# Collecting the outputs of a decode block in one PSUM bank, with one copy, a four-row store and a VectorE transpose for the second layer norm

## The chip, the cores and the metric

The kernel runs on one core of one Trainium2 chip. The metric is the device time of an execution in microseconds (us), and the median over several executions is quoted. "Span" is the time from the first to the last recorded event of the core in the trace. It is about 1.8 us less than the device time. The effects in this study are about 1 us in 410, so every ratio below is between executions on the same chip in the same session; the profiles, and a few times that are said to be of another session, come from several chips.

In the profile PE is TensorE, the matrix unit, and PEld its loads of the stationary operand; DVE is VectorE, ACT ScalarE, POOL GpSimd, and SP issues the transfers (DMA), which 16 DMA engines carry out. PSUM is the memory, of 128 partitions in banks, into which PE adds up its products. The "granted clock" is the share of its full clock that PE was given. LN2 is the second layer norm. A transfer has "landed" when the last of its completion signals is recorded in the trace.

## The reference

It is one decode step (one token) of a transformer block: a layer norm, attention over a cache of 65,536 positions, the residual, a second layer norm, and a gated feed-forward network. All inputs are bf16.

```python
B, Sq, D = 1, 1, 1024
Hq, Hkv, Sk, Dh = 32, 4, 65536, 128        # attention
F = 3584                                   # feed-forward
x = A_x
h  = x + attention(layernorm(x), k_cache, v_cache, wq, wo)      # o @ wo
hn = layernorm(h)
h2 = h + (gelu(hn @ w_gate) * (hn @ w_up)) @ w_down
return h2                                  # (1, 1, 1024) bf16
```

## The kernel before

Keys, values and weights are streamed through a ring of large buffers by one DMA queue, in a fixed order. `w_down` comes last, in five pieces of 14, 7, 4, 2 and 1 "chunks". A chunk is 128 rows of `w_down`, 256 KB. The change touches what happens after the attention projection, and the end.

A product with `w_down` can be laid out in two ways. As a *wide row*, the activation vector is the stationary operand and the weights move through PE, so the 1024 outputs lie along the free dimension of a few partitions. As *columns*, each 128x128 block of weights is loaded as the stationary operand and one column comes out, so the outputs lie across 128 partitions. The kernel used wide rows for the first 21 chunks, spread over four column groups of 32 so that four chunks add up side by side, and columns for the last seven. It joined the two by summing over partitions with one-column matmuls against a vector of ones, which also turns a row into columns.

```python
def row_mm(banks, stat, w2, c, first, last):          # wide row: chunk c in column group c % 4
    g = c % 4
    for s in range(DS):                               # DS = 2 halves of 512 columns
        mm(banks[s][32 * g:32 * g + 32, :], stat, w2[:, s * 512:(s + 1) * 512], first, last,
           loaded=(s > 0), tile_position=(0, 32 * g)) # the second half reuses the loaded weights
# ... attention output rows -> at_ps, copied to at_r [128, 2, 512] f32 ...
hc_ps = ps_t.tile([P, DC], F32, name="hc_ps", tag="T")
for s in range(DS):
    for c in range(DC):                               # 16 column sums: LN2's layout (p c)
        mm(hc_ps[64 * s:64 * s + 64, c:c + 1], at_r[:, s, c::DC], ones_f[:, 0:1], True, True,
           tile_position=(0, 64 * s))
h_pc = const.tile([P, DC], F32, name="h_pc")
nc.vector.tensor_tensor(out=h_pc[:], in0=hc_ps[:], in1=x_pc[:], op=ALU.add)
hn_bf = const.tile([P, DC], BF16, name="hn_bf")
layernorm_cols(h_pc[:], hn_bf[:], "ln2")
hnz = padded(rows, hn_bf[:], DC, "hnz")

def cp_sum(row, add, name):                           # 16 column sums: the output's layout (c p)
    ps = ps_t.tile([P, 4, DS], F32, name=name + "_ps", tag="T")
    for b in range(4):
        for s in range(DS):
            mm(ps[:, b, s:s + 1], row[:, s, b * P:(b + 1) * P], ones_f[:, 0:1], True, True)
    # ... the sums plus `add`, as t [128, 8] ...
h_cp = cp_sum(at_r, x_cp, "h_cp")
# ... gate and up products (they need hnz), GELU -> act_bf [128, 28] ...
sizes = [14, 7, 4, 2, 1]
NW = 21
for sz in sizes:
    wv = load(wd_v[:, c0:c0 + sz, :], "wd_sb")
    for cc in range(sz):
        c = c0 + cc
        if c < NW:
            row_mm(d_ps, actz[:, c, :], wv[:, cc, :], c, c < 4, c + 4 >= NW)
            continue
        for j in range(DC):                           # the last 7 chunks as columns
            mm(dl_ps[:, j:j + 1], wv[:, cc, j * P:(j + 1) * P], act_bf[:, c:c + 1], False, False,
               skip_group_check=True)
    c0 += sz
    if c0 == NW:                                      # rows of 21 chunks -> columns
        d_r = rows.tile([P, DS, 512], F32, name="d_r")
        for s in range(DS):
            evac(d_r[:, s, :], d_ps[s][:], s)
        hd_cp = cp_sum(d_r, h_cp, "hd_cp")
nc.vector.tensor_tensor(out=o_col[:], in0=dl_ps[:], in1=hd_cp[:], op=ALU.add)
oT_ps = ps_t.tile([DC, P], BF16, name="oT_ps", tag="T")
tr(oT_ps[:], o_col[:], ident_bf[:])                   # transpose on PE: [128, 8] -> [8, 128]
o_row = rows.tile([DC, P], BF16, name="o_row")
nc.vector.tensor_copy(out=o_row[:], in_=oT_ps[:])
nc.sync.dma_start(out=out[0, 0].rearrange("(c p) -> c p", p=P), in_=o_row[:])
```

Of the kernel before, what the change touches and what calls it, by code (L numbers as in the profile page):

```python
# [9 lines left out]
ALU = mybir.AluOpType  # L10
AX = mybir.AxisListType
BF16 = mybir.dt.bfloat16
F32 = mybir.dt.float32
PSUM = bass.MemoryType.PSUM
# [3 lines left out]
def kernel(  # L18
# [13 lines left out]
    nc = tc.nc  # L32
    P = 128
    D = A_x.shape[-1]
# [3 lines left out]
    rep = Hq // Hkv  # L38
    F = B_w_gate.shape[1]
    DC = D // P  # L40
    FC = F // P
# [13 lines left out]
    NS = Hkv * 4  # L55
    W0 = 32
# [3 lines left out]
    lead = ctx.enter_context(tc.tile_pool(name="lead", bufs=1))  # L60
    ones_f = lead.tile([P, P], F32, name="ones_f")
# [2 lines left out]
    sel = lead.tile([P, 32], F32, name="sel")  # L64
    hmask = lead.tile([P, rep], F32, name="hmask")
    x_pc = lead.tile([P, DC], F32, name="x_pc")
    x_cp = lead.tile([P, DC], F32, name="x_cp")
    x_row = lead.tile([DC, P], BF16, name="x_row")
    ident_bf = lead.tile([P, P], BF16, name="ident_bf")
    x_pc_bf = lead.tile([P, DC], BF16, name="x_pc_bf")  # L70
    xn_bf = lead.tile([P, DC], BF16, name="xn_bf")
    neg_half = lead.tile([P, 1], F32, name="neg_half")
    oT_all = lead.tile([P, Hq], BF16, name="oT_all")
    used = sum(-(-b // 32) * 32 for b in (4 * P, 4 * P, 2 * (W0 + NS * P), 128, 4 * rep, 4 * DC, 4 * DC, 2 * P, 2 * P,
                                          2 * DC, 2 * DC, 4, 2 * Hq))
    lead.tile([P, (-(used + 128)) % 4096], mybir.dt.uint8, name="lead_pad")
    chpool = ctx.enter_context(tc.tile_pool(name="chpool", bufs=NBUF))
# [46 lines left out]
    def mm(out, lhsT, rhs, start, stop, loaded=False, tile_position=None, skip_group_check=False):  # L124
        t = nc.tensor
        if not loaded:
            return pe(t.matmul(out, lhsT=lhsT, rhs=rhs, start=start, stop=stop, tile_position=tile_position,  # L127
                               skip_group_check=skip_group_check))
        op = t.add_instruction(mybir.InstMatmult(  # L129
            name=nc.get_next_instruction_name(), engine=t.engine, start_tensor_calc=start, stop_tensor_calc=stop,  # L130
            tile_size=(lhsT.shape[0], lhsT.shape[1]), tile_position=tile_position or (0, 0), ldweights=False,
            bass_skip_group_check=skip_group_check,
            ins=[t.lower_ap(rhs), t.lower_ap(lhsT, for_matmul_weights=True)], outs=[t.lower_ap(out, opt=True)]))
        reuses.add(op.ins.name)
        return pe(op)

    def tr(out, in_, identity):
        pe(nc.tensor.transpose(out=out, in_=in_, identity=identity))  # L138
# [9 lines left out]
    WB = max(1, CW // HD)  # L148
    assert HD <= CW and DC % WB == 0
    nc.scalar.dma_start(out=x_pc_bf[:], in_=A_x[0, 0].rearrange("(p c) -> p c", c=DC))  # L150
    nc.scalar.dma_start(out=x_row[:], in_=A_x[0, 0].rearrange("(c p) -> c p", p=P))
    wq_tiles = []
    for c0 in range(0, DC, WB):
        wv = load(wq_v[:, c0:c0 + WB, :], "wq_sb")
# [40 lines left out]

    nc.vector.tensor_copy(out=x_pc[:], in_=x_pc_bf[:])
    layernorm_cols(x_pc[:], xn_bf[:], "ln1")
    xT_ps = ps_m.tile([P, DC], BF16, name="xT_ps", tag="misc")
    tr(xT_ps[:], x_row[:], ident_bf[0:DC, 0:DC])
    nc.vector.tensor_copy(out=x_cp[:], in_=xT_ps[:])  # L200

    def padded(pool, vec, ncols, name, tag=None):
        t = pool.tile([P, ncols, 32], BF16, name=name, tag=tag or name)
        nc.gpsimd.memset(t[:], 0.0)
        nc.vector.tensor_copy(out=t[:, :, 0], in_=vec)
        return t
# [7 lines left out]
    def evac(dst, src, k):  # L214
        if k % 2 == 0:
            nc.vector.tensor_copy(out=dst, in_=src)  # L216
        else:
            nc.scalar.copy(out=dst, in_=src)
# [175 lines left out]
    actx.close()  # L394
    rows = ctx.enter_context(tc.tile_pool(name="rows", bufs=1))
    ps_w = ctx.enter_context(tc.tile_pool(name="ps_w", bufs=4, space=PSUM))
    ps_t = ctx.enter_context(tc.tile_pool(name="ps_t", bufs=3, space=PSUM))
    DS = D // 512

    def row_bank(name):  # L400
        return ps_w.tile([P, 512], F32, name=name, tag="w")

    def row_mm(banks, stat, w2, c, first, last):
# [3 lines that stand above are left out]
               loaded=(s > 0), tile_position=(0, 32 * g))  # L407
# [6 lines left out]
    for wc in range(Hq // WN):  # L414
        wv = load(wo_v[:, wc * WN:(wc + 1) * WN, :], "wo_sb")
        for cc in range(WN):
            c = wc * WN + cc
            row_mm(at_ps, o2z[:, c, :], wv[:, cc, :], c, c < 4, c + 4 >= Hq)
    at_r = rows.tile([P, DS, 512], F32, name="at_r")
    for s in range(DS):  # L420
        evac(at_r[:, s, :], at_ps[s][:], s)
    hc_ps = ps_t.tile([P, DC], F32, name="hc_ps", tag="T")
    for s in range(DS):
        for c in range(DC):
            mm(hc_ps[64 * s:64 * s + 64, c:c + 1], at_r[:, s, c::DC], ones_f[:, 0:1], True, True,
               tile_position=(0, 64 * s))
    h_pc = const.tile([P, DC], F32, name="h_pc")
    nc.vector.tensor_tensor(out=h_pc[:], in0=hc_ps[:], in1=x_pc[:], op=ALU.add)
    hn_bf = const.tile([P, DC], BF16, name="hn_bf")
    layernorm_cols(h_pc[:], hn_bf[:], "ln2")  # L430
    hnz = padded(rows, hn_bf[:], DC, "hnz")

    def cp_sum(row, add, name):
        ps = ps_t.tile([P, 4, DS], F32, name=name + "_ps", tag="T")
        for b in range(4):
            for s in range(DS):
                mm(ps[:, b, s:s + 1], row[:, s, b * P:(b + 1) * P], ones_f[:, 0:1], True, True)
        t = rows.tile([P, DC], F32, name=name)
        nc.vector.tensor_tensor(out=t[:].rearrange("p (s b) -> p b s", b=4), in0=ps[:],
                                in1=add[:].rearrange("p (s b) -> p b s", b=4), op=ALU.add)  # L440
        return t

    h_cp = cp_sum(at_r, x_cp, "h_cp")

    assert F <= CW and FC == 28
    GB = CW // F
# [55 lines left out]

    wd_v = B_w_down.rearrange("(p c) n -> p c n", p=P)
    sizes = [14, 7, 4, 2, 1]
    NW = 21
    assert sum(sizes) == FC
    actz = padded(rows, act_bf[:, 0:NW], NW, "actz")
    d_ps = [row_bank("d_ps") for _ in range(DS)]
    dl_ps = ps_m.tile([P, DC], F32, name="dl_ps", tag="misc")
    nc.vector.memset(dl_ps[:], 0.0)  # L510
    o_col = rows.tile([P, DC], BF16, name="o_col")
    c0 = 0
    for sz in sizes:
        wv = load(wd_v[:, c0:c0 + sz, :], "wd_sb")
        for cc in range(sz):
            c = c0 + cc
            if c < NW:
                row_mm(d_ps, actz[:, c, :], wv[:, cc, :], c, c < 4, c + 4 >= NW)
                continue
            for j in range(DC):  # L520
                mm(dl_ps[:, j:j + 1], wv[:, cc, j * P:(j + 1) * P], act_bf[:, c:c + 1], False, False,
                   skip_group_check=True)
        c0 += sz
        if c0 == NW:
            d_r = rows.tile([P, DS, 512], F32, name="d_r")
            for s in range(DS):
                evac(d_r[:, s, :], d_ps[s][:], s)
            hd_cp = cp_sum(d_r, h_cp, "hd_cp")
    nc.vector.tensor_tensor(out=o_col[:], in0=dl_ps[:], in1=hd_cp[:], op=ALU.add)
    oT_ps = ps_t.tile([DC, P], BF16, name="oT_ps", tag="T")  # L530
    tr(oT_ps[:], o_col[:], ident_bf[:])
    o_row = rows.tile([DC, P], BF16, name="o_row")
    nc.vector.tensor_copy(out=o_row[:], in_=oT_ps[:])
    nc.sync.dma_start(out=out[0, 0].rearrange("(c p) -> c p", p=P), in_=o_row[:])


# [28 lines left out]
```

## Time and profile before

| what | value |
|---|---|
| time, first three executions | 410.66 us (410.0 to 410.76) |
| time of the profiled execution | 411.24 us |
| span of the profiled execution | 409.5 us |
| data read | 173.02 MB |
| last weights landed (estimate below) | about 404.1 us |
| last weights landed to end of span | 5.3 us |

The load queue q1 is busy for 98.1% of the span, so the kernel is bound by data, except at its end.

The transfers view of the kernel before has one line for each kind of transfer, with its size and its time from issue to landing.

```profile
wd_sb<-in_B_w_down_dram SPq DMA_DIRECT2D x1, 256.0 KB, 13.3
```

This is the last piece of `w_down`. It was issued at 390.83 us, so it landed at about 404.1. The windows view of the kernel before agrees. Its columns are: the window and its length; busy time of PE, PEld, DVE, ACT and POOL with counts of instructions; the granted PE clock; the DMA share; and GB/s.

```profile
403.00:404.00 1.00, 1.00 (x6) 1.00 (x6) 0.00 (x0) 0.00 (x0) 0.00 (x0) 0.50 0.34 131
404.00:405.00 1.00, 1.00 (x8) 1.00 (x8) 0.00 (x0) 0.00 (x0) 0.00 (x0) 0.50 0.00 0
```

No data moves after 404, but PE is fully busy. The timeline of the kernel before shows with what. Each line has the start, the duration, the engine, source line and operation, output and input, count, and, in brackets, the idle time before it and what ended that.

```profile
366.72 0.18 DVE L205 COPY hnz<-hn_bf 128x8 bf16<-128x8 bf16 x1
...
370.35 1.04 PE L129 MATMUL wu_ps<-wu_sb,hnz 128*32 128x512 bf16 x7 [2.25 <-DMA wu_sb<-in_B_w_up_dram]
...
400.98 0.69 DVE L216 COPY d_r<-d_ps 128x512 f32<-128x512 f32 x1 [7.95 <-PE d_ps L129]
...
401.72 3.36 PE L127 MATMUL hd_cp_ps<-ones_f,d_r 128*128 128x1 f32 x16 [0.79 <-DVE d_r L216]
...
404.95 1.63 PE L127 MATMUL dl_ps<-act_bf,wd_sb 128*128 128x1 bf16 x56
...
406.62 0.17 DVE L529 TENSOR_TENSOR o_col<-dl_ps,hd_cp 128x8 bf16<-128x8 f32 x1 [1.32 <-PE dl_ps L127]
...
406.84 0.27 PE L138 MATMUL oT_ps<-ident_bf,o_col 128*8 128x128 bf16 x1 [0.26 <-DVE o_col L529]
407.14 0.21 DVE L533 COPY o_row<-oT_ps 8x128 bf16<-8x128 bf16 x1 [0.36 <-PE oT_ps L138]
407.44 0.37 SPq L534 DMA_DIRECT2D out_dram<-o_row  x1
```

The 16 column sums hold PE for 3.36 us and the 56 last matmuls queue behind them. PE is therefore late for the last weights, and the store is issued 3.3 us after they landed.

### The profile page before, as it was taken

How to read it: one execution, taken by the hardware profiler on the slowest of the kernel's cores; microseconds unless marked ns; L12 is line 12 of the kernel's file. 1: busy time of each engine (PE TensorE's matmuls, PEld its weight loads, DVE VectorE, ACT ScalarE, POOL GpSimd, SP SyncE). 2: the span in 40 equal slices, each digit the busy share in tenths (PEclk: the TensorE clock that was granted, in tenths of full speed). 3: DMA queues.
4: the chain of work that ended last, by engine and by line, in shares of the span. 5: the costliest groups of instructions: out<-in, count | busy, mean ns of one | idle time of the engine just before them, and what ended most of it. 6: DMA issues, size and time to landing. Idle time of an engine off the chain costs nothing.

```text
span 409.5 us, 2725 instructions
## 1 busy us (share of the span) xinstructions
PE 307.7 (75%) x1521; PEld 70.6 (17%) x732; DVE 202.6 (49%) x189; ACT 45.5 (11%) x68; POOL 7.2 (2%) x17
## 2 busy tenths in 40 slices
PE   0356397769997788898966869977867997875666
PEld 0111011111110111111111121110112111360224
DVE  1118989876683678646464958182753001110111
ACT  1010000050000041000002220000051000000000
POOL 2000000000000000000000000000010000100000
PEclk9965778969999989899989998999768899866666
DMA  8999999999999999999999999999999999999993
GB/s 359 410 461 410 453 416 442 427 439 432 415 451 416 455 411 451 419 448 423 439 431 426 445 414 450 419 445 423 448 423 434 435 426 445 419 432 429 439 413 151
DMA packets 6669, 173.20 MB, mean 423 GB/s; under 512 B 896, under 2 KB 896, under 8 KB 1152
## 3 DMA queue, kind: packets, MB, share of 16 engines
q1 hardware_dynamic: 6496, 173.02, 98.1%
q8 instruction: 9, 0.15, 0.1%
q10 hardware_dynamic: 160, 0.00, 0.0%
q14 instruction: 4, 0.03, 0.0%
HBM read 173.02 MB, written 0.00 MB: 423 GB/s over the span
## 4 chain that ended last, share of the span: by engine, by line
DMA 46%; PE 30%; DVE 18%; ACT 4%; issue 2%; SPq 0%; ACTq 0%; DVEq 0%
DMA k_sb<-in_A_k_cache_dram 32%; DVE k_sb L259 12%; PE acc_ps L129 10%; DMA wu_sb<-in_B_w_up_dram 8%; DMA wd_sb<-in_B_w_down_dram 6%; PE qk_ps L127 6%; PE qk_ps L129 6%; PE acc_ps L127 4%; DVE mx L280 2%; ACT sc L279 2%; DVE pT L304 1%; ACT pe_r L301 1%; PE o_ps L127 1%; DVE acc_sb L330 1%; ACT acc_sb L332 1%
## 5 line engine op out<-in xcount | busy, mean ns | idle before, releaser
L259 DVE STREAM_TRANSPOSE k_sb<-k_sb 128x2048 uint32<-128x2048 uint32 x64 | 142.1, 2278 | 33.8 <-DMA k_sb<-in_A_k_cache_dram 33.8
L127 PE MATMUL qk_ps<-k_sb,wsel 128*128 128x512 bf16 x256 | 104.7, 409 | 37.5 <-DVE k_sb L259 25.2
L129 PE MATMUL acc_ps<-v_sb,pT 128*128 128x512 bf16 x384 | 111.3, 401 | 0.0
L129 PE MATMUL qk_ps<-k_sb,wsel 128*128 128x512 bf16 x256 | 104.2, 407 | 0.0
L127 PE MATMUL acc_ps<-v_sb,pT 128*128 128x512 bf16 x128 | 51.4, 402 | 0.0
L127 PEld LDWEIGHTS <-wsel 128*128 128x128 bf16 x256 | 26.1, 102 | 143.4 <-issue 123.7
L280 DVE TENSOR_REDUCE mx<-qk_ps 128x1 f32<-128x1024 f32 x16 | 19.5, 1220 | 44.9 <-ACT sc L279 44.9
L279 ACT COPY sc<-qk_ps 128x1024 f32<-128x1024 f32 x16 | 16.2, 1012 | 201.9 <-PE qk_ps L129 201.9
L127 PEld LDWEIGHTS <-pT 128*128 128x128 bf16 x128 | 13.6, 106 | 98.3 <-issue 98.2
L304 DVE STREAM_TRANSPOSE pT<-pe_r 128x1024 bf16<-128x1024 bf16 x16 | 19.0, 1227 | 6.2 <-ACT pe_r L301 6.2
L330 DVE COPY acc_sb<-acc_ps 32x512 f32<-32x512 f32 x8 | 5.4, 672 | 32.8 <-PE acc_ps L129 32.7
L301 ACT ACTIVATE pe_r<-sc,nbias 128x1024 bf16<-128x1024 f32 x16 | 18.2, 1140 | 14.3 <-DVE nbias L296 13.5
L332 ACT COPY acc_sb<-acc_ps 32x512 f32<-32x512 f32 x8 | 4.6, 578 | 62.0 <-DVE acc_sb L330 61.9
L127 PE MATMUL q_ps<-wq_sb,xnz 128*32 128x512 bf16 x32 | 5.2, 625 | 7.9 <-DMA wq_sb<-in_A_wq_dram 7.9
L127 PE MATMUL ln_tot<-ln_s,ones_f 128*128 128x1 f32 x8 | 2.3, 352 | 10.8 <-DVE ln_s L177 8.9
L127 PE MATMUL o_ps<-sel,acc_sb 128*128 128x8 f32 x32 | 5.1, 288 | 6.7 <-DVE rl L344 5.9
L138 PE MATMUL mxT_ps<-ident_f,mx 128*1 128x128 f32 x4 | 1.3, 321 | 10.8 <-DVE mx L285 10.8
L127 PE MATMUL wg_ps<-wg_sb,hnz 128*32 128x512 bf16 x32 | 6.4, 591 | 3.8 <-DMA wg_sb<-in_B_w_gate_dram 3.1
L129 PE MATMUL wu_ps<-wu_sb,hnz 128*32 128x512 bf16 x40 | 7.3, 586 | 2.3 <-DMA wu_sb<-in_B_w_up_dram 2.3
L216 DVE COPY wg_ev<-wg_ps 128x512 f32<-128x512 f32 x1 | 0.7, 692 | 14.9 <-PE wg_ps L127 14.9
L216 DVE COPY q_ev<-q_ps 128x512 f32<-128x512 f32 x1 | 0.7, 692 | 14.0 <-PE q_ps L129 14.0
L127 PE MATMUL d_ps<-wd_sb,actz 128*32 128x512 bf16 x21 | 3.4, 538 | 4.0 <-DMA wd_sb<-in_B_w_down_dram 4.0
(116 smaller groups left out, 110.6 us busy)
## 6 DMA issues: line engine op xcount, KB each, us to landing
k_sb<-in_A_k_cache_dram SPq DMA_DIRECT2D x16, 4096.0 KB, 33.7
v_sb<-in_A_v_cache_dram SPq DMA_DIRECT2D x16, 4096.0 KB, 36.8
wq_sb<-in_A_wq_dram SPq DMA_DIRECT2D x2, 4096.0 KB, 16.7
wo_sb<-in_A_wo_dram SPq DMA_DIRECT2D x2, 4096.0 KB, 30.3
wg_sb<-in_B_w_gate_dram SPq DMA_DIRECT2D x2, 3584.0 KB, 31.6
wu_sb<-in_B_w_up_dram SPq DMA_DIRECT2D x2, 3584.0 KB, 32.7
wd_sb<-in_B_w_down_dram SPq DMA_DIRECT2D x1, 3584.0 KB
wd_sb<-in_B_w_down_dram SPq DMA_DIRECT2D x1, 1792.0 KB, 24.6
```

Source lines behind the costliest of these rows:

```text
L127: return pe(t.matmul(out, lhsT=lhsT, rhs=rhs, start=start, stop=stop, tile_position=tile_position, skip_group_check=skip_group_check))
L129: op = t.add_instruction(mybir.InstMatmult(name=nc.get_next_instruction_name(), engine=t.engine, start_tensor_calc=start, stop_tensor_calc ...
L138: pe(nc.tensor.transpose(out=out, in_=in_, identity=identity))
L216: nc.vector.tensor_copy(out=dst, in_=src)
L259: dv(nc.vector.transpose(out=kt[:, c * w:(c + 1) * w], in_=kt[:, c * w:(c + 1) * w]))
L279: ac(nc.scalar.copy(out=sc[:], in_=flat))
L280: dv(nc.vector.tensor_reduce(out=state[("mx", g)][:, li:li + 1], in_=flat, axis=AX.X, op=ALU.max))
L301: ac(nc.scalar.activation(out=pe_r[:], in_=state.pop(("sc", g, li))[:], func=ACT.Exp, bias=nbias[:, 0:1], scale=scale, accum_out=lpart[:, ...
L304: dv(nc.vector.transpose(out=pT[:].rearrange("p m c -> p (m c)"), in_=pe_r[:]))
L330: dv(nc.vector.tensor_copy(out=acc_sb[sl, :], in_=acc[sl, c, :]))
L332: ac(nc.scalar.copy(out=acc_sb[sl, :], in_=acc[sl, c, :]))
```

## The change

The intent is that all output contributions accumulate in one bank `f_ps` of 128x256. Column group g (partitions 32g to 32g+31) holds outputs 256g to 256g+255, with the useful row on its first partition. The attention rows enter by four matmuls against ones. The residual enters by matmuls that select a row of `x`. Every chunk of `w_down` enters by four matmuls of 256 columns. At the end there is one copy and one store of partitions 0, 32, 64 and 96. The second layer norm takes its input from the same bank by a VectorE transpose. The column sums, their copies and the PE transpose go away.

```diff
-    x_row = lead.tile([DC, P], BF16, name="x_row")
+    x_row = lead.tile([4, D // 4], BF16, name="x_row")
 ...
-    # hc_ps: 16 column sums, h_pc = hc_ps + x_pc
+    OW = D // 4
+    f_ps = ps_f.tile([P, OW], F32, name="f_ps")
+
+    def out_mm(stat, mov, first, last, groups=range(4)):
+        for g in groups:
+            mm(f_ps[32 * g:32 * g + 32, :], stat, mov(g), first, last, tile_position=(0, 32 * g),
+               skip_group_check=True)
+
+    out_mm(ones_f[:, 0:32], lambda g: at_r[:, g // 2, g % 2 * OW:g % 2 * OW + OW], True, False)
+    for g in range(4):
+        out_mm(ident_bf[0:4, g:g + 32], lambda g: x_row[:], False, False, groups=[g])
+    h_t = rows.tile([P, DC, 32], F32, name="h_t")
+    nc.vector.transpose(out=h_t[:].rearrange("p c j -> p (c j)"), in_=f_ps[:].rearrange("p (i c) -> p c i", c=DC))
-    layernorm_cols(h_pc[:], hn_bf[:], "ln2")
+    layernorm_cols(h_t[:, :, 0], hn_bf[:], "ln2")
 ...
-    # cp_sum and h_cp = cp_sum(at_r, x_cp, "h_cp")
 ...
-    actz = padded(rows, act_bf[:, 0:NW], NW, "actz")
+    actz = padded(rows, act_bf[:], FC, "actz")
 ...  for each chunk:
-            # row_mm into d_ps (c < 21), or 8 column matmuls into dl_ps
+            out_mm(actz[:, c, :], lambda g: wv[:, cc, g * OW:(g + 1) * OW], False, c + 1 == FC)
-    # d_r, hd_cp, o_col, PE transpose, o_row, store of 8 rows of 128
+    o_fin = rows.tile([P, OW], BF16, name="o_fin")
+    nc.vector.tensor_copy(out=o_fin[0:97, :], in_=f_ps[0:97, :])
+    nc.sync.dma_start(out=out[0, 0].rearrange("(g n) -> g n", n=OW), in_=o_fin[0:97:32, :])
```

More of the change, by code (lines that the diff above doesn't have):

```diff
@@ L66 @@
     x_pc = lead.tile([P, DC], F32, name="x_pc")
-    x_cp = lead.tile([P, DC], F32, name="x_cp")
-    x_row = lead.tile([DC, P], BF16, name="x_row")
+    x_row = lead.tile([4, D // 4], BF16, name="x_row")
     ident_bf = lead.tile([P, P], BF16, name="ident_bf")
@@ L73 @@
     oT_all = lead.tile([P, Hq], BF16, name="oT_all")
-    used = sum(-(-b // 32) * 32 for b in (4 * P, 4 * P, 2 * (W0 + NS * P), 128, 4 * rep, 4 * DC, 4 * DC, 2 * P, 2 * P,
+    used = sum(-(-b // 32) * 32 for b in (4 * P, 4 * P, 2 * (W0 + NS * P), 128, 4 * rep, 4 * DC, D // 2, 2 * P,
                                           2 * DC, 2 * DC, 4, 2 * Hq))
@@ L150 @@
     nc.scalar.dma_start(out=x_pc_bf[:], in_=A_x[0, 0].rearrange("(p c) -> p c", c=DC))
-    nc.scalar.dma_start(out=x_row[:], in_=A_x[0, 0].rearrange("(c p) -> c p", p=P))
+    nc.scalar.dma_start(out=x_row[:], in_=A_x[0, 0].rearrange("(g n) -> g n", g=4))
     wq_tiles = []
@@ L197 @@
     layernorm_cols(x_pc[:], xn_bf[:], "ln1")
-    xT_ps = ps_m.tile([P, DC], BF16, name="xT_ps", tag="misc")
-    tr(xT_ps[:], x_row[:], ident_bf[0:DC, 0:DC])
-    nc.vector.tensor_copy(out=x_cp[:], in_=xT_ps[:])
     def padded(pool, vec, ncols, name, tag=None):
@@ L396 @@
     ps_w = ctx.enter_context(tc.tile_pool(name="ps_w", bufs=4, space=PSUM))
-    ps_t = ctx.enter_context(tc.tile_pool(name="ps_t", bufs=3, space=PSUM))
+    ps_t = ctx.enter_context(tc.tile_pool(name="ps_t", bufs=2, space=PSUM))
+    ps_f = ctx.enter_context(tc.tile_pool(name="ps_f", bufs=1, space=PSUM))
     DS = D // 512
@@ L421 @@
         evac(at_r[:, s, :], at_ps[s][:], s)
-    hc_ps = ps_t.tile([P, DC], F32, name="hc_ps", tag="T")
-    for s in range(DS):
-        for c in range(DC):
-            mm(hc_ps[64 * s:64 * s + 64, c:c + 1], at_r[:, s, c::DC], ones_f[:, 0:1], True, True,
-               tile_position=(0, 64 * s))
-    h_pc = const.tile([P, DC], F32, name="h_pc")
-    nc.vector.tensor_tensor(out=h_pc[:], in0=hc_ps[:], in1=x_pc[:], op=ALU.add)
+    OW = D // 4
[4 more added lines that the diff above has]
+               skip_group_check=True)
+    assert OW == 32 * DC
+    out_mm(ones_f[:, 0:32], lambda g: at_r[:, g // 2, g % 2 * OW:g % 2 * OW + OW], True, False)
[3 more added lines that the diff above has]
+    nc.vector.transpose(out=h_t[:].rearrange("p c j -> p (c j)"), in_=f_ps[:].rearrange("p (i c) -> p c i", c=DC))
     hn_bf = const.tile([P, DC], BF16, name="hn_bf")
-    layernorm_cols(h_pc[:], hn_bf[:], "ln2")
+    layernorm_cols(h_t[:, :, 0], hn_bf[:], "ln2")
     hnz = padded(rows, hn_bf[:], DC, "hnz")
-    def cp_sum(row, add, name):
-        ps = ps_t.tile([P, 4, DS], F32, name=name + "_ps", tag="T")
-        for b in range(4):
-            for s in range(DS):
-                mm(ps[:, b, s:s + 1], row[:, s, b * P:(b + 1) * P], ones_f[:, 0:1], True, True)
-        t = rows.tile([P, DC], F32, name=name)
-        nc.vector.tensor_tensor(out=t[:].rearrange("p (s b) -> p b s", b=4), in0=ps[:],
-                                in1=add[:].rearrange("p (s b) -> p b s", b=4), op=ALU.add)
-        return t
-    h_cp = cp_sum(at_r, x_cp, "h_cp")
     assert F <= CW and FC == 28
@@ L504 @@
     sizes = [14, 7, 4, 2, 1]
-    NW = 21
     assert sum(sizes) == FC
-    actz = padded(rows, act_bf[:, 0:NW], NW, "actz")
-    d_ps = [row_bank("d_ps") for _ in range(DS)]
-    dl_ps = ps_m.tile([P, DC], F32, name="dl_ps", tag="misc")
-    nc.vector.memset(dl_ps[:], 0.0)
-    o_col = rows.tile([P, DC], BF16, name="o_col")
+    actz = padded(rows, act_bf[:], FC, "actz")
     c0 = 0
@@ L516 @@
             c = c0 + cc
-            if c < NW:
-                row_mm(d_ps, actz[:, c, :], wv[:, cc, :], c, c < 4, c + 4 >= NW)
-                continue
-            for j in range(DC):
-                mm(dl_ps[:, j:j + 1], wv[:, cc, j * P:(j + 1) * P], act_bf[:, c:c + 1], False, False,
-                   skip_group_check=True)
-        c0 += sz
-        if c0 == NW:
-            d_r = rows.tile([P, DS, 512], F32, name="d_r")
-            for s in range(DS):
-                evac(d_r[:, s, :], d_ps[s][:], s)
-            hd_cp = cp_sum(d_r, h_cp, "hd_cp")
-    nc.vector.tensor_tensor(out=o_col[:], in0=dl_ps[:], in1=hd_cp[:], op=ALU.add)
-    oT_ps = ps_t.tile([DC, P], BF16, name="oT_ps", tag="T")
-    tr(oT_ps[:], o_col[:], ident_bf[:])
-    o_row = rows.tile([DC, P], BF16, name="o_row")
-    nc.vector.tensor_copy(out=o_row[:], in_=oT_ps[:])
-    nc.sync.dma_start(out=out[0, 0].rearrange("(c p) -> c p", p=P), in_=o_row[:])
+            out_mm(actz[:, c, :], lambda g: wv[:, cc, g * OW:(g + 1) * OW], False, c + 1 == FC)
+        c0 += sz
+    o_fin = rows.tile([P, OW], BF16, name="o_fin")
+    nc.vector.tensor_copy(out=o_fin[0:97, :], in_=f_ps[0:97, :])
+    nc.sync.dma_start(out=out[0, 0].rearrange("(g n) -> g n", n=OW), in_=o_fin[0:97:32, :])
 _INS = ['A_x', 'A_k_cache', 'A_v_cache', 'A_wq', 'A_wo', 'B_x', 'B_w_gate', 'B_w_up', 'B_w_down']
```

## The prediction

> **What bounds the kernel now.** Data transfer, then a serial tail. The page shows the DMA queue busy for 98.1% of 16 engines' span (173 MB at 423 GB/s; span 409.5 us). The transfer table gives the last down-weight load (256 KB, issued 390.83 us) 13.3 us to land, so the last weights are there at about 404.1 us; the windows by microsecond show 131 GB/s in 403-404 and nothing in 404-405. The span ends 5.4 us later. Only that tail, and delays of the loads, can change the time.
>
> **The tail before** (timeline): d_r copies 400.98-401.67; 16 column sums hd_cp 401.72-405.08; the 56 dl_ps matmuls of the last 7 chunks, which queue behind them, 404.95-406.58; o_col, transpose and o_row copy to 407.35; store issued 407.44, end 409.46 (2.02 us after). PE is late by the column sums; the last load is not waited for.
>
> **What the change does there.** Removed: the d_r copies (0.69), hd_cp (3.36), its add (0.17), the dl_ps matmuls (1.63), o_col, the transpose, o_row. Added: 28 chunks of 4 column-tiled matmuls of 256 columns, each with its own weight load (112 loads, 21 before); one 97x256 copy from PSUM.
> Does PE keep up? Before, a chunk's two 512-column matmuls took 0.21 us at the low clock (8 in 0.86 us), half that at the high one. Columns are as many, so I estimate 0.21-0.32 us a chunk even with 4 loads. The pieces of 14, 7, 4, 2, 1 chunks land near 395.6, 399.9, 402.3, 403.5, 404.1: 14 chunks need 3-4.5 us of the 4.2 there, so PE is nearly idle when the last chunk lands. The Trainium skill ("TensorE: Matmul & The Clock Gate", "Step-by-step") says PE pulls weight loads ahead of running matmuls; this trace agrees (dl_ps: a load and a matmul every 29 ns).
> After the last landing: 0.03 wait + 0.40 for loads and 4 matmuls + 0.04 + copy 0.43 (estimate, from 0.17 for 8 columns and 0.69 for 512) + 0.09 + 2.02 store = 3.0 us. The store is 4 rows of 512 B, not 8 of 256 B; [...]so no gain there. End: 404.1 + 3.0 = 407.1 against 409.5: **-2.3 us**.
>
> **LN2.** Removed: 32 hc_ps sums (3.55) and 16 h_cp sums (3.55), which held back hn_bf. Added: 4 f32 matmuls of 256 columns, 4 small bf16 ones, a 128x256 vector transpose (estimate 0.45, from 2.28 for 2048). hnz is ready 4-5 us earlier than 366.9. It buys nothing: after the first 7 gate matmuls PE waits for wu_sb, which lands at 370.24, and the loads are issued as before, with the queue always full.
>
> **Prediction.** 408.3 us, 8 in 10 between 407.4 and 409.2. Faster by over 2%: 0.01; within 2%: 0.98; slower by over 2%: 0.01.
>
> **Signs it is right.** The last down load lands at 404.1 +-0.4; the final f_ps matmul starts within 0.4 us of it with DMA wd_sb as its releaser; copy near 0.43; store issued near 405.1; tail after the last landing about 3 us; hnz near 362.
>
> **What would make it wrong.** If the 4 loads per chunk do not hide (0.5-0.6 us a chunk at the low clock), PE falls behind from the first piece, ends up to 5 us late, and the gain is lost. A longer store, or a drift of the load rate by 0.3%, is half of the gain.

## More of the kernel before

The page of the kernel before shows the busy time of each engine, then the DMA queues: packets, megabytes, and share of the span of 16 DMA engines.

```profile
span 409.5 us, 2725 instructions
...
PE 307.7 (75%) x1521; PEld 70.6 (17%) x732; DVE 202.6 (49%) x189; ACT 45.5 (11%) x68; POOL 7.2 (2%) x17
...
q1 hardware_dynamic: 6496, 173.02, 98.1%
q8 instruction: 9, 0.15, 0.1%
```

The line q8 looks negligible: nine transfers of instructions, 16 KB each.

## The result, and the profile after

| | before | after |
|---|---|---|
| median us (range, executions) | 410.71 (410.0 to 411.49, 4) | 409.6 (409.52 to 409.78, 4) |
| ratio after/before, 95% interval | | 0.9973, 0.9955 to 0.9992 |
| span of the profiled execution | 409.5 | 407.7 |

The change made the kernel 1.1 us faster (0.3 to 1.8 by the interval), where 2.3 was predicted, and 409.6 us lies outside the predicted range of 407.4 to 409.2.

The page of the kernel after:

```profile
span 407.7 us, 2657 instructions
...
PE 298.5 (73%) x1481; PEld 62.8 (15%) x713; DVE 201.9 (50%) x183; ACT 44.9 (11%) x67; POOL 7.4 (2%) x17
...
q1 hardware_dynamic: 6488, 173.02, 98.6%
q8 instruction: 8, 0.13, 0.1%
```

The timeline of the kernel after:

```profile
358.32 0.45 DVE L432 STREAM_TRANSPOSE h_t<-f_ps 128x256 f32<-128x256 f32 x1 [0.96 <-PE f_ps L126]
...
361.84 0.18 DVE L201 COPY hnz<-hn_bf 128x8 bf16<-128x8 bf16 x1
...
370.37 1.04 PE L128 MATMUL wu_ps<-wu_sb,hnz 128*32 128x512 bf16 x7 [7.15 <-DMA wu_sb<-in_B_w_up_dram]
...
395.76 3.18 PE L126 MATMUL f_ps<-wd_sb,actz 128*32 128x256 bf16 x56 [2.99 <-DMA wd_sb<-in_B_w_down_dram]
...
400.01 0.95 PE L126 MATMUL f_ps<-wd_sb,actz 128*32 128x256 bf16 x28 [1.07 <-DMA wd_sb<-in_B_w_down_dram]
...
403.66 1.02 PE L126 MATMUL f_ps<-wd_sb,actz 128*32 128x256 bf16 x12 [0.20 <-DMA wd_sb<-in_B_w_down_dram]
...
404.73 0.42 DVE L507 CAST o_fin<-f_ps 97x256 bf16<-97x256 f32 x1 [11.46 <-PE f_ps L126]
405.24 0.65 SPq L508 DMA_DIRECT2D out_dram<-o_fin  x1
```

The end went as intended. PE waits for each piece (the releasers are loads of `wd_sb`), it is done at 404.68, 0.44 us after the last landing at 404.24, and the copy takes 0.42 us. The layer norm's result `hnz` is ready 4.9 us earlier, but the 7 `wu_ps` matmuls start at 370.37, as they did at 370.35 before, because both kernels wait there for the same weights. What PE gained it spends waiting: 7.15 us idle where there were 2.25.

From one profiled execution to the other the time shrank by 1.7 us (411.24 to 409.52), but over all executions by 1.1. The comparison of two single profiles is thus itself off. The store's issue also takes 0.65 us, where the old one took 0.37.

### The profile page after: what moved, and what is told of

The parts are those of the page before. It is cut to its first block, busy times and chain, and to the rows that moved or that the text cites. A ratio compares the mean times of both kernels' runs of the same rounds, so it can differ in the third digit from the quotient of the medians. Undisturbed runs are those within 1.5% of the kernel's fastest.

```text
span 407.7 us, 2657 instructions
## 1 busy us (share of the span) xinstructions
PE 298.5 (73%) x1481; PEld 62.8 (15%) x713; DVE 201.9 (50%) x183; ACT 44.9 (11%) x67; POOL 7.4 (2%) x17
## 4 chain that ended last, share of the span: by engine, by line
DMA 45%; PE 30%; DVE 18%; ACT 4%; issue 2%; SPq 0%; ACTq 0%; DVEq 0%
DMA k_sb<-in_A_k_cache_dram 32%; DVE k_sb L255 12%; PE acc_ps L128 12%; DMA wg_sb<-in_B_w_gate_dram 8%; PE qk_ps L126 6%; PE qk_ps L128 6%; DMA wd_sb<-in_B_w_down_dram 5%; PE acc_ps L126 4%; DVE mx L276 2%; ACT sc L275 2%; DVE pT L300 1%; ACT pe_r L297 1%; PE o_ps L126 1%; DVE acc_sb L326 1%; ACT acc_sb L328 1%
## 5 line engine op out<-in xcount | busy, mean ns | idle before, releaser
L126 PE MATMUL f_ps<-wd_sb,actz 128*32 128x256 bf16 x112 | 6.2, 377 | 5.7 <-DMA wd_sb<-in_B_w_down_dram 5.7
L126 PEld LDWEIGHTS <-hnz 128*32 128x32 bf16 x48 | 2.7, 129 | 23.4 <-issue 21.8
```

Source lines behind the costliest of these rows:

```text
L126: return pe(t.matmul(out, lhsT=lhsT, rhs=rhs, start=start, stop=stop, tile_position=tile_position, skip_group_check=skip_group_check))
```

## The experiments

The theory had two parts. (C) The 3.36 us of column sums, read from one execution, were not typical. (S) The new store, from partitions 32 apart, is slower than the old one; its rival (R) is that the size or number of its rows makes it so. Another rival was that one half of the change has a cost that the other half hides. The kernels below were made to tell these apart.

### The two kernels again, and each half of the change alone

`e1_before_again` is the kernel before and `e2_after_again` the kernel after, both unchanged. `e3_tail_only` is the kernel after with the old input to the layer norm:

```diff
+    hc_ps = ps_t.tile([P, DC], F32, name="hc_ps", tag="T")        # the 16 old column sums
+    ...
+    nc.vector.tensor_tensor(out=h_pc[:], in0=hc_ps[:], in1=x_pc[:], op=ALU.add)
     # f_ps as in the kernel after
-    h_t = ...; nc.vector.transpose(out=h_t..., in_=f_ps...)
-    layernorm_cols(h_t[:, :, 0], hn_bf[:], "ln2")
+    layernorm_cols(h_pc[:], hn_bf[:], "ln2")
```

`e4_ln2_only` is the kernel before with the new input to the layer norm and the old end:

```diff
-    # hc_ps, h_pc
+    # f_ps from at_r and x_row4, h_t by nc.vector.transpose, as in the kernel after
-    layernorm_cols(h_pc[:], hn_bf[:], "ln2")
+    layernorm_cols(h_t[:, :, 0], hn_bf[:], "ln2")
```

Expected:

> The kernel before, unchanged, against itself: a control. Ratio 1.000 within 0.002. What is asked is how far its own end wanders. Theory A (the profile of before that I predicted from was an ordinary one, the loss is all in the changed kernel): last down-weight landing near 404.1 us of its span, tail after it 5.3 us, span near 409.5. Theory B (that profile was one of a longer run, 411.24 against a median of 410.7, so part of the missing 1.2 us was never there): span 408.5 to 409.2, with either an earlier landing or a shorter tail. Store: issue 0.37 us, issue start to landing 1.2 us.

> The changed kernel, unchanged, with more rounds, to get a firmer gain. Theory A (a slower store costs 0.45 us of the 2.3): gain 1.6 to 2.0 us. Theory B (part of the gain was a long run of before): gain 1.0 to 1.4 us. If the slow store is a property of the store and not of that one execution, its issue again takes 0.6 to 0.7 us and issue start to landing 1.65 us. x_pc_bf landed 5 us later than in before (13.1 against 8.1); if that is chance it will differ here.

> The changed kernel with the old LN2 input (32 column sums, add): only the end of the change. All theories that put the gain in the tail: same time as the changed kernel within 0.3 us, hnz near 366 us instead of 362, store slow as in the changed kernel.

> The kernel before with only the new LN2 input (row gather, vector transpose); the old end is kept. My prediction: ratio 1.000 within 0.002, hnz earlier by some us, wg/wu waits longer, nothing at the end. Rival: an earlier LN2 does help by freeing a buffer sooner; then 0.5 us or more faster.

Measured, against 410.72 us (409.64 to 412.38, 11 executions) of the kernel before in the same session:

| kernel | median us (range, n) | ratio, 95% interval |
|---|---|---|
| before again | 410.82 (409.89 to 411.30, 6) | 0.9998, 0.9979 to 1.0016 |
| after again | 409.52 (409.31 to 409.94, 6) | 0.9970, 0.9952 to 0.9988 |
| new end only | 410.97 (409.86 to 411.05, 6) | 1.0000, 0.9983 to 1.0018 |
| new layer norm input only | 411.22 (410.35 to 412.69, 6) | 1.0012, 0.9992 to 1.0033 |

The result repeats: 1.2 us (0.5 to 2.0 by the interval), which is theory B of `e2`. The profile of `e1` was again one of a long execution (411.25 us; span 409.5). The late landing of `x_pc_bf` that `e2` asked about is not of the change: it took 12.3 us from issue in both repeats, and 7.3 us only in the first profile. The kernel before scatters over 2.7 us in 11 executions, the kernel after over 0.6 us in six. The second half alone gains nothing, as predicted, although its `hnz` was ready at 362.26 us. But the new end alone gained nothing either, which nobody had expected. Five of its six spans were 409.1 or 409.2 us and one was 408.0. So it has short executions like those of the kernel after, and long ones of 1.1 us more, which are the usual ones. The timeline of the new end alone:

```profile
403.70 0.62 PE L126 MATMUL f_ps<-wd_sb,actz 128*32 128x256 bf16 x8 [0.21 <-DMA wd_sb<-in_B_w_down_dram]
...
405.65 0.41 PE L126 MATMUL f_ps<-wd_sb,actz 128*32 128x256 bf16 x4 [1.33 <-DMA wd_sb<-in_B_w_down_dram]
...
406.10 0.42 DVE L512 CAST o_fin<-f_ps 97x256 bf16<-97x256 f32 x1 [12.56 <-PE f_ps L126]
```

PE waits 1.33 us for the last piece, which became complete at 405.61 us. In the trace 15 DMA engines had finished by 404.29, and one completed its share 1.3 us later. The queues in the transfers view of the same kernel, from 403 to 406 us, show what else ran there (the kernels before and after have only the first of these lines in that window):

```profile
q1 hardware_dynamic: 80, 0.14, 12.0%
q8 instruction: 1, 0.02, 2.0%
```

An instruction fetch of 16 KB, recorded as one packet of 0.95 us, fell into the last microseconds. The counts of fetches follow the number of PE instructions: the kernel after has 1481 matmuls and 713 weight loads recorded and eight fetches, the new end alone has 1513 and 745 and nine. This gave a theory (F) for the missing gain of the half: its 64 extra PE instructions bring a ninth fetch that delays the last weights. The rival (L) was that its layer norm, 2.1 us later than in the kernel after, delays the end.

### A dose of PE instructions, and the store's shape

`e5_pad64` and `e6_pad16` add 64 and 16 idle PE instructions (32 and 8 matmuls, each with a weight load) to the kernel after, where PE has time:

```diff
     hnz = padded(rows, hn_bf[:], DC, "hnz")
+    pad_ps = ps_m.tile([P, 1], F32, name="pad_ps", tag="misc")
+    for _ in range(32):        # 8 in pad16
+        mm(pad_ps[0:32, :], ident_bf[:, 0:32], ident_bf[:, 0:1], True, True)
```

`e7_store_contig` and `e8_store_8rows` store the same number of bytes from neighbouring partitions, in 4 rows of 512 bytes or 8 of 256. Their outputs are wrong, which doesn't matter for the times.

```diff
-    nc.sync.dma_start(out=out[0, 0].rearrange("(g n) -> g n", n=OW), in_=o_fin[0:97:32, :])
+    nc.sync.dma_start(out=out[0, 0].rearrange("(g n) -> g n", n=OW), in_=o_fin[0:4, :])       # e7
+    nc.sync.dma_start(out=out[0, 0].rearrange("(g n) -> g n", n=P), in_=o_fin[0:8, 0:P])      # e8
```

> The changed kernel plus 32 one-column matmuls with their weight loads (64 PE instructions, result never read), placed in the 8 us in which PE waits for wu_sb: as many PE instructions as the tail-only version has. Theory F (a 16 KB fetch of PE instructions falls just before the last weights land and holds one DMA engine for about 1 us): a ninth fetch appears near 403.6 us, the last landing moves from 404.2-404.5 to about 405.5, and the time goes to about 411.0, as in the tail-only version. Rival L (the tail-only version was slow because of its old, later LN2 input): no change, 409.5.

> The same with 8 such matmuls (16 PE instructions), too few to need a ninth fetch. Both theories: 409.5 us, 8 fetches, last landing 404.2 to 404.5. If it is slow too, it is the dummy matmuls themselves that cost, and the theory of the fetch falls.

> The changed kernel with a store of 4 rows of 512 B from four neighbouring partitions (0 to 3) in place of partitions 0, 32, 64, 96. Wrong result on purpose. Theory S (the partition step of 32 makes the issue long): issue back to about 0.37 us, store start to landing 1.2 us, time 0.4 to 0.5 us less than the changed kernel (about 409.1). Rival R (512 B rows, or the number of rows, makes it long): issue stays 0.65 us, same time as the changed kernel.

> The changed kernel with the old store shape: 8 rows of 256 B from partitions 0 to 7. Wrong result on purpose. Theories S and R both: issue 0.36 us, start to landing 1.2 us, time about 409.1. If the issue stays 0.65, what is slow is not the shape of the store.

Measured, against 410.53 us (410.12 to 411.58, 11) of the kernel before:

| kernel | median us (range, n) | ratio, 95% interval | fetches |
|---|---|---|---|
| after + 64 PE instructions | 409.81 (409.63 to 411.03, 6) | 0.9984, 0.9971 to 0.9998 | 9 |
| after + 16 PE instructions | 409.48 (409.39 to 410.53, 6) | 0.9978, 0.9965 to 0.9991 | 8 |
| store of 4 neighbouring rows | 409.12 (408.88 to 409.39, 5) | 0.9964, 0.9952 to 0.9976 | |
| store of 8 neighbouring rows | 409.08 (408.96 to 409.42, 6) | 0.9963, 0.9951 to 0.9975 | |

The count of fetches obeyed theory F, but the time obeyed it in only one of six executions: five spans of 64 added instructions were 407.9 or 408.1 us and one was 409.3. In the profile, one of the fast ones, the ninth fetch lies where it was expected, at 403.54, but the last weights landed at 404.35 and PE did not wait. The timeline of this kernel:

```profile
403.76 1.03 PE L126 MATMUL f_ps<-wd_sb,actz 128*32 128x256 bf16 x12 [0.20 <-DMA wd_sb<-in_B_w_down_dram]
```

So theory F as it was put failed here: the same fetch does not always delay the end. The records do not name the engine on which a fetch runs (the packets looked at further below tell more).

The store experiments are clear. These are the issues in the timelines of the two kernels, first four and then eight neighbouring rows:

```profile
405.53 0.34 SPq L508 DMA_DIRECT2D out_dram<-o_fin  x1
```

```profile
405.51 0.37 SPq L508 DMA_DIRECT2D out_dram<-o_fin  x1
```

The issue takes 0.34 and 0.37 us where 0.65 was seen with a step of 32 partitions. From the start of the issue to the last landing it takes 1.19 us with four neighbouring rows, and 1.67 us in the kernel after (405.24 to 406.91). The time is 0.4 us below that of the kernel after with 16 idle instructions in the same session, and below the 409.5 and 409.6 us of the kernel after in the other two. The kernel after itself was not run beside them. The size and the number of rows make no difference, but the step between partitions does; 32 and 1 are the only steps tried. Why the step costs time, no run shows.

### The sums taken away, two stores, and moving the fetch

`e10_before_no_sums` tests part C: it is the kernel before without its last column sums (a wrong result).

```diff
-        if c0 == NW:
-            d_r = rows.tile([P, DS, 512], F32, name="d_r")
-            for s in range(DS):
-                evac(d_r[:, s, :], d_ps[s][:], s)
-            hd_cp = cp_sum(d_r, h_cp, "hd_cp")
-    nc.vector.tensor_tensor(out=o_col[:], in0=dl_ps[:], in1=hd_cp[:], op=ALU.add)
+    nc.vector.tensor_tensor(out=o_col[:], in0=dl_ps[:], in1=h_cp[:], op=ALU.add)
```

`e9_tail_only_pad64` adds the 64 idle instructions to the new end alone, to move the ninth fetch to before the last weights.

```diff
     hnz = padded(rows, hn_bf[:], DC, "hnz")
+    for _ in range(32):        # in the kernel of e3
+        mm(pad_ps[0:32, :], ident_bf[:, 0:32], ident_bf[:, 0:1], True, True)
```

`e11_two_stores` is a version with a right result that avoids the step. Groups 0 and 2 get their useful row on their last partition and groups 1 and 3 on their first, so that partitions 31, 32 and 95, 96 are neighbours. Two queues store them.

```diff
-    actz = padded(rows, act_bf[:], FC, "actz")
+    actz = rows.tile([P, FC, 64], BF16, name="actz")
+    nc.gpsimd.memset(actz[:], 0.0)
+    nc.vector.tensor_copy(out=actz[:, :, 31], in_=act_bf[:])
 ...
-            out_mm(actz[:, c, :], lambda g: wv[:, cc, g * OW:(g + 1) * OW], False, c + 1 == FC)
+            for g in range(4):
+                o = 31 * (g % 2)
+                out_mm(actz[:, c, o:o + 32], lambda g: wv[:, cc, g * OW:(g + 1) * OW], False, c + 1 == FC, groups=[g])
 ...
-    nc.sync.dma_start(out=out[0, 0].rearrange("(g n) -> g n", n=OW), in_=o_fin[0:97:32, :])
+    out_v = out[0, 0].rearrange("(g n) -> g n", n=OW)
+    nc.sync.dma_start(out=out_v[0:2], in_=o_fin[31:33, :])
+    nc.scalar.dma_start(out=out_v[2:4], in_=o_fin[95:97, :])
```

(The residual is selected into all 32 rows of each group, and the copy covers all 128 partitions.) `e12_two_stores_split` also halves the copy between two engines:

```diff
-    nc.vector.tensor_copy(out=o_fin[:], in_=f_ps[:])
+    nc.vector.tensor_copy(out=o_fin[:, 0:OW // 2], in_=f_ps[:, 0:OW // 2])
+    nc.scalar.copy(out=o_fin[:, OW // 2:], in_=f_ps[:, OW // 2:])
```

> The tail-only version (old LN2 input, new end; it measured like the kernel before) plus 64 PE instructions in the wait for wu_sb, so that the ninth fetch of PE instructions comes 64 instructions (8 chunks) earlier. Theory F (the fetch collides with the end of the last loads): fetch between 399 and 402 us, last landing 404.2 to 404.6, time back to 409.5 to 409.9. Rival L (the old, later LN2 input costs the time): stays at 411.0.

> The kernel before without the copies of d_r and the 16 column sums hd_cp and their add (the first 21 chunks' result is dropped: wrong on purpose). It measures what these were worth in an average execution. In the profile I predicted from they took 4.05 us, and PE would then wait for the last load and end about 2.1 us earlier. Theory C (that profile caught them at PE's low clock; on average PE is faster there): gain on the kernel before 1.3 to 1.7 us, and the spread of the runs shrinks from over 1.5 us to under 0.6 us. Rival (their cost is the same in every execution): gain 2.0 us or more, spread unchanged.

> A version with the right result whose four output rows lie in two pairs of neighbouring partitions (31, 32 and 95, 96), stored by two queues at once, two rows each. Theory S (the partition step makes the issue long): issue 0.34 to 0.37 us on each queue, 0.3 to 0.4 us faster than the changed kernel: about 409.1, and about 1.5 us faster than the kernel before.

> The same, with the last copy split by columns between VectorE and ScalarE (128 columns each, estimate 0.30 us in place of 0.42). About 0.1 us faster than the two-store version, about 409.0; this is less than the runs spread.

Measured, against 411.08 us (410.17 to 412.51, 9) of the kernel before:

| kernel | median us (range, n) | ratio, 95% interval |
|---|---|---|
| new end only + 64 PE instructions | 410.61 (410.58 to 411.18, 5) | 0.9999, 0.9986 to 1.0011 |
| before without the sums | 409.33 (409.21 to 409.60, 5) | 0.9966, 0.9953 to 0.9978 |
| two stores | 409.17 (409.08 to 409.25, 5) | 0.9961, 0.9949 to 0.9974 |
| two stores, copy halved | 409.27 (409.14 to 409.37, 5) | 0.9963, 0.9950 to 0.9977 |

Without the sums the kernel before gains 1.4 us (0.34% of 411; 0.9 to 1.9 by the interval), where the first profile promised about 2.1, and its scatter falls from 2.3 us to 0.4. The sums are thus worth less than that profile said, and they are what makes the kernel before vary. The timeline of this kernel has the next step two microseconds earlier than the 406.62 of the first profile:

```profile
404.53 0.17 DVE L524 TENSOR_TENSOR o_col<-dl_ps,h_cp 128x8 bf16<-128x8 f32 x1 [11.77 <-PE dl_ps L127]
```

Moving the fetch failed, so this expectation from theory F was wrong too. It came at 401.27 us, as expected, but the piece of four chunks then arrived late, as the timeline of this kernel shows:

```profile
404.09 1.05 PE L126 MATMUL f_ps<-wd_sb,actz 128*32 128x256 bf16 x16 [1.85 <-DMA wd_sb<-in_B_w_down_dram]
```

The last piece landed at 405.89. The windows view of this kernel shows one DMA engine working alone at the end (0.06 is one sixteenth):

```profile
404.50:405.00 0.50, 0.50 (x12) 0.30 (x5) 0.00 (x0) 0.00 (x0) 0.00 (x0) 0.50 0.06 25
405.00:405.50 0.50, 0.30 (x9) 0.14 (x8) 0.00 (x0) 0.00 (x0) 0.00 (x0) 0.50 0.06 25
```

This was the longest of the five executions (411.18 us; the others took 410.58 to 410.65), and its loads were some 0.5 us late already before the fetch: the piece of seven chunks landed at 400.51, against 399.76 to 400.22 in the other profiles. But one engine was a further 1.1 us later than the others with each of the last three pieces, so a fetch three microseconds before the usual landing went with harm too. The reading that fits is that whatever is queued behind it on its engine becomes late.

Two stores have the lowest time of the versions with a right result, but they were not run beside the kernel after, and the intervals of the two ratios overlap (0.9949 to 0.9974 here, 0.9952 to 0.9988 there). Their issues, in the timeline of that kernel, take about half of the single store's:

```profile
405.11 0.27 ACTq L516 DMA_DIRECT2D out_dram<-o_fin  x1
405.16 0.33 SPq L515 DMA_DIRECT2D out_dram<-o_fin  x1
```

Halving the copy gained nothing. In its timeline the half on ACT ran after the one on DVE, not beside it:

```profile
405.10 0.27 ACT L514 CAST o_fin<-f_ps 128x128 bf16<-128x128 f32 x1 [13.57 <-DVE o_fin L513]
```

### How typical the first profile of before was, and the last rival

`e13_before_look1`, `e14_before_look2` and `e15_before_look3` are looks at the kernel before, unchanged. `e16_tail_only_look` is another look at the new end alone. `e17_late_ln2` tests rival L: it delays the layer norm of the kernel after by six idle VectorE copies and adds no PE instruction.

```diff
+    idle = rows.tile([P, DS, 512], F32, name="idle")
+    for _ in range(6):
+        dv(nc.vector.tensor_copy(out=idle[:], in_=at_r[:]))
-    nc.vector.transpose(out=h_t[:].rearrange("p c j -> p (c j)"), in_=f_ps[:].rearrange("p (i c) -> p c i", c=DC))
+    dv(nc.vector.transpose(out=h_t[:].rearrange("p c j -> p (c j)"), in_=f_ps[:].rearrange("p (i c) -> p c i", c=DC)))
```

> A further profile of the kernel before, unchanged. Theory C (PE's granted clock at the end sets how long the 16 column sums take): the sums take between 1.9 and 3.4 us and differ from profile to profile; where they take about 2 us the span is 408.0 to 408.7, where they take over 3 us it is 409.0 to 409.6. Rival: the sums take 3.1 to 3.4 us every time, and the span differs for another reason (the landing of the loads).

> As the look before it: a profile of the kernel before; theory C as there. One more point for column sums against span.

> As the two looks before it: a profile of the kernel before; theory C as there. One more point for column sums against span.

> A second profile of the tail-only version, five of whose six runs took 1.2 us longer than its fastest. Theory F: where the span is about 409.1, the ninth fetch of PE instructions lies between 403.4 and 404.6 us and one of the 16 DMA engines completes the last piece at about 405.5, over 1 us after the others; where the span is about 408.0, it does not. Rival: a span of 409.1 with the last landing near 404.3, the time lost elsewhere.

> The changed kernel with six idle VectorE copies (128x1024) ahead of the LN2 transpose, so that hnz is ready several us later, near the 366 us of the tail-only version, with not one PE instruction more. Theory F (only the number of PE instructions, through the late fetch, slowed the tail-only version): 8 fetches, last landing 404.2 to 404.5, time 409.5 as the changed kernel. Rival L (the late LN2 input itself costs 1.4 us): 411.0.

The looks took 410.8, 410.3 and 410.22 us (before) and 410.92 (new end only). The column sums in the timelines of the repeat of the kernel before and of the three looks, in that order:

```profile
401.93 3.15 PE L127 MATMUL hd_cp_ps<-ones_f,d_r 128*128 128x1 f32 x16 [0.79 <-DVE d_r L216]
```

```profile
401.93 2.71 PE L127 MATMUL hd_cp_ps<-ones_f,d_r 128*128 128x1 f32 x16 [0.79 <-DVE d_r L216]
...
407.00 0.37 SPq L534 DMA_DIRECT2D out_dram<-o_row  x1
```

```profile
402.20 1.95 PE L127 MATMUL hd_cp_ps<-ones_f,d_r 128*128 128x1 f32 x16 [0.79 <-DVE d_r L216]
...
406.50 0.37 SPq L534 DMA_DIRECT2D out_dram<-o_row  x1
```

```profile
401.90 2.17 PE L127 MATMUL hd_cp_ps<-ones_f,d_r 128*128 128x1 f32 x16 [0.79 <-DVE d_r L216]
...
406.42 0.37 SPq L534 DMA_DIRECT2D out_dram<-o_row  x1
```

With the first profile, that makes five: 3.36, 3.15, 2.71, 1.95 and 2.17 us for the same 16 matmuls, with spans of 409.5, 409.5, 409.0, 408.5 and 408.4. The trace records the granted clock in steps of 3.41 us or a multiple of it, and in all five it goes from 1.0 to 0.5 around the sums: at 401.99, 402.43, 402.90, 404.18 and 403.47 us. In that order the sums took 3.36, 3.15, 2.71, 1.95 and 2.17 us: the later the step down, the shorter the sums, without an exception. Within a profile the sums change pace at the step: the starts of neighbouring ones lie 0.11 us apart before it (0.13 for the first) and 0.21 us after it (in `e14` the step falls after the last start, and all lie 0.11 apart). The windows view of `e13`, of these matmuls alone (PE, PEld and DVE, then the granted clock), shows both paces, first before the step at 402.90 and then after it:

```profile
401.93:402.84 0.91, 0.91 (x8) 0.91 (x9) 0.00 (x0) 1.00 0.77 311
403.01:404.29 1.28, 1.28 (x7) 1.28 (x8) 0.00 (x0) 0.50 0.30 115
```

The means are 2.67 us and 409.0 us: the profile that the prediction was read from was at the slow end of a spread of 1.1 us.

The look at the new end alone repeats what the first one showed. PE waits 1.42 us for the last piece, one engine completes its share at 405.64 when the others were done by 404.23, and a ninth fetch begins at 403.65.

The packet records in the traces, which no view prints, tell more. For each of SP's 45 loads there are 16 packets of 4 bytes (720 in all, and a few for the store), and nearly all take 9 ns. In the two profiles of the new end alone the last such packet of the last piece starts at 404.54 and 404.59 us, 14 and 15 ns before the end of the fetch, and takes 24 and 25 ns; the other 15 had started by 403.96 and 403.91. So the late share came out just as the fetch ended. That the late engine is the fetch's own is not recorded as such, but the times fit to a few ns in both profiles. `e9` has the same mark: a packet that started 14 ns before the end of its fetch took 0.80 us, where packets of its size took 0.31. In `e5`, whose fetch lasted from 403.54 to 404.47, all 16 packets had started by 404.02, so nothing of the last piece was left behind the fetch. Not explained is what follows: the landing was recorded 1.05 and 1.07 us after that last packet, where 0.3 to 0.4 us is usual.

The kernel with the late layer norm took 409.48 us (409.38 to 409.58, 5), ratio 0.9970 (0.9957 to 0.9984): the full gain. The line of its layer norm in its timeline, and then that of the new end alone:

```profile
364.50 0.18 DVE L201 COPY hnz<-hn_bf 128x8 bf16<-128x8 bf16 x1
```

```profile
363.92 0.18 DVE L201 COPY hnz<-hn_bf 128x8 bf16<-128x8 bf16 x1
```

It has its layer norm at 364.50, later than the new end alone (363.92), and eight fetches. Rival L falls: a late layer norm alone costs nothing. Whether it takes part together with the ninth fetch is untested, because `e17` has the one and `e5` the other.

## Why the prediction was wrong

The prediction took a span of 409.5 before and expected 407.1 after. Two terms of that sum failed: the span it started from, which the column sums of one long execution had stretched, and the store. The terms of that sum, against the profiled execution of the kernel after:

| term | predicted | measured |
|---|---|---|
| last weights landed | 404.1 | 404.24 |
| to the end of the last matmul | 0.43 | 0.44 |
| to the end of the copy | 0.47 | 0.47 |
| to the issue of the store | 0.09 | 0.09 |
| issue of the store to the end | 2.02 | 2.50 |
| end of the span, after | 407.1 | 407.7 |
| end of the span, before | 409.5 | 409.0 (mean of five profiles) |

**The column sums, "hd_cp (3.36)", were mis-sized.** The figure was right for the execution that was read, but the mean of five is 2.67 us, and the spans that go with it average 0.5 us less than the 409.5 that was used as the start. The record had this in reach: the profiled execution took 411.24 us, and the prediction took a gain that was read from it off the median, 410.66. Taking the sums out gains 1.4 us, and it removes the scatter. The sums take their duration from where the step of the clock falls: 0.11 us each before it, 0.21 after. The new kernel has little left for that step to stretch: its executions lie within 0.6 us. The Trainium skill ("TensorE: Matmul & The Clock Gate", "What's actually happening") describes the window as 3413 ns long and free-running. This trace agrees with the length, 3.41 us between records. The cause of the moving step, that the window is free-running, rests on the page and on the five positions here; no run set the phase.

**"2.02 store" and "so no gain there" were wrong: the new store is 0.4 to 0.5 us slower.** The prediction carried the old store's time over and looked only at the size of its rows. In 2.02 us, 1.19 were from issue to landing (407.44 to 408.63) and 0.83 were from landing to the end of the span, which is the same in both kernels. With the source partitions 32 apart the first part became 1.67 us. Neighbouring partitions, in four or eight rows, brought the issue back to 0.34 to 0.37 us, and the time down by 0.4. The prediction had also leaned on the Trainium skill ("DMA: Bandwidth & Descriptors", "Anatomy of one DMA"), whose fixed 2.0 us is given for transfers issued by GpSimd, while SP issued these. That the old store ended 2.02 us after its issue was a coincidence, since 0.83 of it is not transfer.

**The rest is small.** The last weights landed at 404.24 rather than 404.1, about 0.1 us. Together 2.3 - 0.5 - 0.5 - 0.1 = 1.2 us, where 1.1 and 1.2 were measured; the intervals are wider than a fit this close.

**What was right.** The last load bounds the end: the releaser of PE's last waits is the DMA. PE keeps pace with four weight loads a chunk: 14 chunks took 3.18 us (0.23 a chunk), seven took 0.95 at the full clock. The copy was 0.42 for the estimated 0.43. The LN2 half buys no time on its own: `hnz` came 4.9 us earlier, and e4 was no faster. The sign and the class (within 2%) were right.

**What the prediction did not see.** Its account treats the two halves as independent, and says that the LN2 half buys nothing. Alone that is so, but the new end without it gained nothing either. Beside the new end, the LN2 half takes away 64 PE instructions, counted with their loads, and with them a ninth instruction fetch. In both profiles of the new end alone one DMA engine, by the packets the one with that fetch, was late with the last weights by 1.3 and 1.4 us; five of its six spans are as long. The old end could not show it, because its ninth fetch came at 405.4 to 406.4 us, after all loads. Shown are: the fetch and the one late engine in three profiles (e3, e16 and, with the fetch earlier, e9), the fewer fetches with fewer instructions, and that a late layer norm without added PE instructions costs nothing. That the fetches are PE's is inferred from the counts, on average about 259 recorded PE instructions for each (196 to 318 from one to the next in the first profile). That the late engine is the fetch's own is read from packets that fit to a few ns, in e3, e16 and e9. Open is why the landing came 1 us after the last packet, and what decides whether a share of the last piece is still behind the fetch: as far as the spans tell, that was so in five of six executions of e3, but in one of six of e5.

## What to carry to other kernels

A single profile of a kernel whose last microseconds are PE work fixes a span that moves with the clock: look at several executions, or at the range of the times, before subtracting from it, and expect a change that removes such work to gain the mean and to take away the scatter. When a store is the last thing, keep its source rows on neighbouring partitions (here worth 0.4 us), and count the landing and what follows it apart. When a change and its halves do not add up, compare the small queues too: one instruction fetch among the last loads went here with a loss as large as the whole change's gain.

## What the Trainium skill lacked or had wrong

- "Runtime: NRT & Kernel Launch", "Instruction fetch mechanics", has blocks of 16 KiB or 256 instructions, which agrees (16 KB, about 259 recorded PE instructions a fetch). It calls the cost of crossing a block mostly hidden. Here a fetch among the last loads lasted 0.95 us, and the last weights came 1.3 and 1.4 us after the other engines' shares, 0.3% of the time (the link is read from the packets' times, and the fetch does not always do harm).
- "DMA: Bandwidth & Descriptors" does not have the cost of a step between source partitions in a small store: 0.65 us of issue and 1.67 to landing from partitions 32 apart, against 0.34 to 0.37 and 1.19 from neighbours. Its 2.0 us fixed cost stands under the path through GpSimd; these stores, from SP's queue, landed after 1.19 us, or 1.67 with the step.
- "TensorE: Matmul & The Clock Gate", "What's actually happening", puts the penalty of the clock's ramp under 1% of a typical span. What moved here is of that size (1.1 us of 410 between the five profiles of the kernel before, 0.3%), but where the change itself is worth 0.3%, the position of the step decides what one profile shows: 1.95 to 3.36 us for the same 16 matmuls.
- The same page, "The mechanism", has a list by which a weight load overlaps with matmuls in flight only where the row group differs, although its text before the list also allows a load into a background buffer. Here the rows are the same and only the column groups differ, and by the records the loads overlapped: 28 loads (0.75 us of them busy) and 28 matmuls of 256 columns together took 0.95 us, 34 ns for each pair. The line in the list is too narrow for this case.
